# A frequency filter and gated FFN on one core: batch 0's D turned in SBUF, half of batch 1's A through DRAM, x chunks in the first x's buffers

## The chip, the cores and the metric

The kernel runs on one core of a Trainium2 chip. The metric is the device time of one execution in microseconds. All times within an execution are microseconds from the start of the profiled span. The engines are called PE (TensorE, matmul), DVE (VectorE), ACT (ScalarE), POOL (GpSimd) and SP (SyncE, which here only issues DMAs). [...]

## The reference

x has 8 batches of 3008 rows and 256 columns. Each batch is filtered in the frequency domain along its rows, and the 24064 filtered rows go through a gated feed-forward layer with 1536 hidden columns:

```python
X = np.fft.rfft(x, axis=1)                    # x: (8, 3008, 256)
Y = X * (filt_r + 1j * filt_i)[None, :, :]
y = np.fft.irfft(Y, n=3008, axis=1)
t = y.reshape(24064, 256)
out = (np.maximum(t @ w_gate, 0.0) * (t @ w_val)) @ w_out
```

## The kernel before

**The filter as matmuls.** A row number is split, 3008 = N1 x N2 = 94 x 32. The transform of a batch has four stages. *A* is a transform over the 94 values for each of the 32 others; its result must then be turned, so that the 32 values lie along the partitions. The turned A is the tile `at`. `fwd(b, i)`, i from 0 to 5, takes `at` through the second transform (`F2`) into `psX`; `product` multiplies with the filter (`Ftr`, `Fti`) into `tt` and `uu`; `inv(b, i)` goes back through `I2t` and `I2u` into `psD`, and ACT copies that out as *D*. D must be turned as well, with the 94 frequencies' rows (96, `NROW`) on the partitions: the tiles `dC`. `item_c(k, h)` multiplies `dC` with `M1` (the way back over the 94) and gives `yT`, 512 columns of filtered x, transposed, for block k and half h of the 256 columns.

**How the two turns are done.** D goes to DRAM (`Dbuf`) as it stands and is read back in the other order: `inv` sends a DMA at the cuts 0, 2, 4, 6 (for batch 0 also 5), `load_d` reads it in four pieces z, two DMAs each. A of batches 2 to 7 is made by `tiled_a` from x chunks and goes through DRAM too (`Abuf`, `load_at_tiled`). A of batches 0 and 1 is made by `first_a` in 16 items (p, s, h), each one matmul in float32 (two instructions in the profile) and ACT's copy into `AS`, and turned by DVE with `turn_a`, in 32 x 32 blocks of 32-bit words (L301, STREAM_TRANSPOSE).

**The x chunks.** For a batch from 2 on, `load_chunk(b, j)` loads a quarter of x on POOL's queue into `XP[j]`, `fold_chunk` adds and subtracts its halves on POOL, `tiled_a(b, j)` transforms it. `XP` is four tiles of their own, cleared by POOL at step 2 (`clear_chunks`); `fold_chunk` keeps two of its four results in the tile `fold` (two buffers). The first x, of batches 0 and 1, is in `XF`, two tiles in the pool `pro`, which is closed ahead of the main loop.

**The FFN and the order.** 47 blocks of 512 rows, 12 steps each, 564 in all. A step is `gv`: two matmul pairs into `psV` and `psG`, ACT's copy `vsb`, DVE's `prod`; and a twelfth of the output stage `o_part` of the block before. The order on every engine is the order of the program. What belongs to the filter is put at the end of steps by `at_step`: `end` is the step five ahead of the `item_c` that first needs batch b (51 for batch 1, 123 for batch 2), and fwd, inv, `load_d`, `tiled_a` and the loads stand at fixed distances from it. `item_c` of the next block stands at the steps 8 and 10 of a block.

**The start.** x of batch 0 is loaded and transformed, the filters are loaded, `first_b` runs batch 0's six fwd, product and inv, with three items of batch 1's `first_a` between (`amid`). Then come 13 more items; on POOL, `hold_gpsimd` (a small copy that waits for what it reads) delays the first half of the gate and value weights (`load_vg`) until an item of batch 1 is copied, and the second half, the output weights (`load_o`) and two pieces of D until the first piece of `dC` has landed. `item_c(0, h)` and the main loop follow.

**PSUM** has eight banks, handed out in turn by `bank` and `done`.

Of the kernel before, what the change touches and what calls it, by code (L numbers as in the profile page):

```python
# [29 lines left out]
N1, N2 = 94, 32  # L30
# [11 lines left out]
def _tables():  # L42
    n1 = np.arange(N1)
    n2 = np.arange(N2)
    p = np.arange(16)
    wa = np.zeros((128, 128))
    part = 4 * (n1 % 32) + n1 // 32
    m1 = np.zeros((NROW, N1))
    f2 = np.zeros((128, NG, 64))
    lo = np.arange(64)  # L50
    lo = 32 * (lo // 32) + 4 * (lo % 8) + lo % 32 // 8
    own = np.zeros((128, 2, 2, 64))
    order = np.arange(64).reshape(2, 32).T.reshape(64)
    for hg in range(48):
        g, a = divmod(hg, 2)
        rows = slice(a * 64, a * 64 + 64)
        e, j = g % 2, 12 * a + g // 2
        rt, rm = 64 * e + j, 48 * e + j
        f = np.zeros((64, 64))
        t = np.zeros((64, 64))  # L60
        u = np.zeros((64, 64))
        k1 = 1 + g + 24 * a if hg != 47 else 0
        th = 2 * np.pi * (((n1 - 23) * k1) % N1) / N1
        wa[part, rt] = np.cos(th)
        if k1 not in (0, 47):
            wa[part, rt + 32] = -np.sin(th)
            m1[rm] = 2.0 * np.cos(th) / S
            m1[rm + 24] = -2.0 * np.sin(th) / S
            k = np.stack([k1 + N1 * p, S - (N1 * (p + 1) - k1)], 1).reshape(32)
            conj = np.tile([1.0, -1.0], 16)  # L70
            th = 2 * np.pi * (np.outer(n2, k) % S) / S
            c, s = np.cos(th), np.sin(th)
            f[:] = np.block([[c, -s], [s, c]])
            ct, st = c.T, s.T
            t[:] = np.block([[ct, st], [-st, ct]])
            u[:] = np.block([[-st, ct], [-ct, -st]]) * np.concatenate([conj, conj])[:, None]
        else:
            m1[rm] = np.cos(th) / S
            th = 2 * np.pi * (np.outer(n2, k1 + N1 * p) % S) / S
            c, s = np.cos(th), np.sin(th)  # L80
            f[0:32, 0:32:2] = c
            f[0:32, 32::2] = -s
            t[0:32:2, 0:32] = 2.0 * c.T
            t[32::2, 0:32] = -2.0 * s.T
            u[0:32:2, 0:32] = -2.0 * s.T
            u[32::2, 0:32] = -2.0 * c.T
            if k1 == 0:
                sign = np.where(n2 % 2 == 0, 1.0, -1.0)
                f[0:32, 32] = sign
                t[0, 0:32] = 1.0  # L90
                t[32, 0:32] = sign
                u[0] = 0.0
                u[32] = 0.0
        f2[lo + 64 * e, j] = f
        if g >= NG - 2:
            own[rows, 0, g - NG + 2], own[rows, 1, g - NG + 2] = t[:, order], u[:, order]

    r = np.arange(128)
    perm = np.zeros((128, 64))
    perm[r, 2 * (8 * (r % 4) + r // 4 % 8) + r // 32 % 2] = 1.0  # L100
    swap = np.zeros((128, 128))
    conj = np.where(r % 2 == 0, 1.0, -1.0)
    swap[r ^ 32, r] = conj * np.where(r & 32, -1.0, 1.0)
    m1 = np.concatenate([m1, np.zeros((128 - NROW, N1))])
    fold = np.zeros((128, 4, 32))
    i = np.arange(24)
    for odd in range(2):
        k1 = 2 - odd + 2 * (i % 12) + 24 * (i // 12)
        if not odd:
            k1[k1 == 48] = 0  # L110
        th = 2 * np.pi * (np.outer(i - 23, k1) % N1) / N1
        half = np.where(i == 23, 0.5, 1.0)[:, None]
        for q in range(4):
            fold[32 * q:32 * q + 24, 2 * odd, 0:24] = np.cos(th) * half
            fold[32 * q:32 * q + 24, 2 * odd + 1, 0:24] = np.where(k1 % 47 == 0, 0.0, -np.sin(th))
    tab = np.concatenate([perm, swap, own.reshape(128, -1), m1], 1)
    return wa.astype(np.float32), fold.reshape(128, 128).astype(np.float32), f2.astype(NBF16), tab.astype(NBF16)
# [3 lines left out]
def kernel(  # L121
# [44 lines left out]
    Abuf = [dram.tile([NROW * N2, D], BF16, name=f"Abuf{b}") if b > 1 else None for b in range(B)]  # L166
    Dbuf = [dram.tile([NROW * N2, D], BF16, name=f"Dbuf{b}") for b in range(B)]

    XF = [pro.tile([128, NX2 * D], FP32, name=f"XF{c}") for c in range(N2 // NX2)]
    WA = pro.tile([128, 128], FP32)  # L170
    AS = [[pro.tile([128, NC2, N2 // NC2, D // 2], BF16, name=f"AS{b}{h}")] for b, h in ((0, 0), (0, 1), (1, 0))]
    WF = consts.tile([128, 4, 32], FP32)
    M1 = consts.tile([NROW, N1], BF16)
# [46 lines left out]
    def place_own():  # L220

        for i, t in enumerate((I2t, I2u)):
            o = 192 + i * 128
            nc.vector.tensor_copy(t[64:, NG - 2:, :],
                                  tabs[64:, o:o + 128].rearrange("p (g n) -> p g n", g=2))
        nc.vector.tensor_copy(M1, tabs[:NROW, 448:])

# [49 lines left out]
    def first_a(b, p, s, h):  # L277
# [6 lines left out]
        if len(AS) == 3 and (b, h) == (1, 1):  # L284
# [7 lines left out]
    def turn_a(b, h, i=0, d0=0, d1=None):  # L292

        if (h, i, d0) == (0, 0, 0):
            ats[b] = sb.tile([128, 32, D], BF16, tag="at", bufs=1, name="at")
# [5 lines left out]
        nc.vector.transpose(dst[:, o + d0:o + d1, :], src[:, d0:d1, :])  # L301

# [15 lines left out]
    def fold_chunk(b, j):  # L318

        xp = XP[j]  # L320
        t = fs.tile([128, 2, 512], FP32, tag="fold", bufs=2, name="fold")
        tt = nc.gpsimd.tensor_tensor
        tt(t, xp[:, 0:2], xp[:, 2:4], op=ALU.add)  # L323
        tt(xp[:, 2:4], xp[:, 0:2], xp[:, 2:4], op=ALU.subtract)  # L324
        tt(xp[:, 0], t[:, 0], t[:, 1], op=ALU.add)
        tt(t[:, 0], t[:, 0], t[:, 1], op=ALU.subtract)
        tt(t[:, 1], xp[:, 2], xp[:, 3], op=ALU.add)
        tt(xp[:, 2], xp[:, 2], xp[:, 3], op=ALU.subtract)
        fold[b, j] = (xp[:, 0], t[:, 0], t[:, 1], xp[:, 2])
# [66 lines left out]
    def inv(b, i, cuts=CUTS):  # L396

        if i in cuts:
            if (b, i) == (0, 5):
                dsb = AS[0][0].rearrange("p (a o) c d -> p a (o c d)", a=2)  # L400
                dsb = dsb.rearrange("p a (o d) -> p a o d", d=D)
            else:
                dsb = sb.tile([128, 2, 4, D], BF16, tag="dsb", bufs=3, name="dsb")
            dsbs[b] = i, dsb
        i0, dsb = dsbs[b]
# [10 lines left out]
        o = 2 * (i - i0)  # L416
        for a in range(2):
            copy = nc.vector.tensor_copy if (b, i, a) == (0, 5, 0) else nc.scalar.copy
            copy(dsb[:, a, o:o + 2, :], psD[a])  # L419
            done(psD[a])  # L420
        if i + 1 in cuts:
            nc.sync.dma_start(_ap(Dbuf[b], 2 * i0 * D, [[NG * D, 128], [NG // 2 * D, 2], [1, (o + 2) * D]]),
                              dsb[:, :, :o + 2, :])

    def first_b(amid):

        cuts = (0, 2, 4, 5, 6)
        for i in range(6):
# [6 lines left out]
            if i > 1:  # L435
                inv(0, i - 2, cuts=cuts)
            amid(i)
        inv(0, 4, cuts=cuts)
        amid(6)
        inv(0, 5, cuts=cuts)  # L440

    dCs = {}

    def load_d(b, z0=0, z1=NZ, engs=(nc.sync, nc.sync)):
        for z in range(z0, z1):
            dC = sb.tile([NROW, 8, D], BF16, tag="dC", bufs=6)
            for e in range(2):
                engs[e].dma_start(dC[48 * e:48 * e + 48],
                                  _ap(Dbuf[b], (64 * e + 16 * z) * NG * D,
                                      [[D, 48], [48 * D, 8], [1, D]]))  # L450
            dCs[b, z] = dC
# [13 lines left out]
    def item_c(k, h):  # L465
# [4 lines left out]
        for (o, b, n2, n1, w) in runs(k * W, W):  # L470
            nc.tensor.matmul(psY[:, o:o + w],  # L471
                             dCs[b, n2 // 8][:, n2 % 8, h * 128:(h + 1) * 128], M1[:, n1:n1 + w],
# [103 lines left out]
    for i in range(3):  # L576
        make_back_u(i)
    for h in range(2):
# [4 lines left out]
    place_filter(1, 0, 0, nc.gpsimd.tensor_copy)  # L583
    for fi, a, half in ((0, 0, 0), (0, 1, 0), (1, 1, 0), (0, 0, 1), (0, 1, 1), (1, 0, 1), (1, 1, 1)):
        place_filter(fi, a, half, nc.sync.dma_start)
    load_x(1, sp, ((0, 0, 2 * q), (0, 2 * q, 4 * q), (1, 0, 2 * q), (1, 2 * q, 4 * q)))
    early = iter([(0, s, h) for h in range(2) for s in range(2)] +
                 [(p, s, h) for h in range(2) for p in range(1, 4) for s in range(2)])

    def amid(i):  # L590
# [4 lines left out]
        for _ in range((0, 0, 0, 0, 1, 1, 1)[i]):  # L595
            first_a(1, *next(early))

    first_b(amid)
    for _ in range(3):
        p, s, h = next(early)  # L600
        first_a(1, p, s, h)
    hold_gpsimd(AS[2][0][:, 4 * s, p, 0:8])
    load_vg(0, DFF // 2)
    load_d(0, 0, 2)
    hold_gpsimd(dCs[0, 0][:, 7, D - 8:])
    load_vg(DFF // 2, DFF)
    load_o()
    load_d(0, 2, 4, (nc.gpsimd, nc.gpsimd))
    for p, s, h in early:
        first_a(1, p, s, h)  # L610
        if (p, s, h) == (3, 1, 0):
            turn_a(1, 0)
    for h in range(2):
        item_c(0, h)
# [3 lines left out]
    XP = []  # L618

    def clear_chunks():  # L620
        for i in range(4):
            XP.append(fs.tile([128, 4, 512], FP32, tag=f"XP{i}", bufs=1, name=f"XP{i}"))
            nc.gpsimd.memset(XP[i], 0.0)

# [6 lines left out]
    for k in range(4):  # L631
        at_step((5, 11, 14, 16)[k], lambda k=k: turn_a(1, 1, k // 2, k % 2 * 16, k % 2 * 16 + 16))
    at_step(2, clear_chunks)
    for b in range(1, B):
        end = (b * S // W - 1) * NFT + C_AT[0] - 5
        if b > 1:
            for j, e in enumerate((-74, -69, -62, -55) if b == 2 else (-74, -69, -64, -57)):
                l = (22, 29, 34, 43)[j] if b == 2 else end - 115 + NFT * j
# [11 lines left out]
        for i in range(7):  # L650
            l = -33 + 5 * i if b == 1 else -40 + 6 * i
# [6 lines left out]
        at_step(end - (1 if b == 1 else 2), lambda b=b: load_d(b))  # L658
# [42 lines left out]
```

## Time and profile before

| | us |
|---|---|
| median of 3 runs (lowest, highest) | 889.12 (887.46, 891.44) |
| the profiled execution | 888.4 |
| its span | 886.3 |
| PE busy, in the span | 863.7 |
| DVE, ACT, POOL busy | 573.8, 500.7, 373.5 |
| the first fwd of batch 0 (psX) | 27.0 |
| the last inv of batch 0 (psD) | 39.0 |
| the first matmul of the FFN (psV) | 53.8 |
| the first fwd of batch 1, step 18 (psX) | 75.2 |
| the last inv of batch 1, step 48 (psD) | 121.3 |

The table of windows gives for a stretch its length, then the busy time of PE, weight load, DVE, ACT and POOL, the granted clock of PE, the DMA share (busy share of the 16 DMA engines; above 1 where several transfers overlap on them) and GB/s. The granted clock was 1.00 in every stretch looked at. In the timeline a line is: start, duration, engine, line, operation, written tile, read tiles, shape, count, and in brackets the engine's idle time before it with what ended it. "SPq" and "POOLq" are the engines' queues of DMA issues: the duration there is that of issuing.

### The profile page before, as it was taken

The page shows a single profiled execution, that of the slowest core. Times are in us where ns is not written, and L with a number is a line of the kernel's source. Part 1 is how long each engine was busy: PE and PEld are TensorE (multiplying, and loading weights), DVE is VectorE, ACT ScalarE, POOL GpSimd, SP SyncE. Part 2 cuts the span into 40 slices and gives each one's busy share as a digit, 9 for nine tenths or more (in the row PEclk, how much of TensorE's full clock was granted, in tenths as well). Part 3 has the DMA queues.
Part 4 walks back from the last instruction along what each step waited for, and adds up shares of the span by engine and source line. Part 5 has one row for each costly group of instructions (what it writes and reads, how often), then busy time and mean ns, then how long its engine had stood idle before and what let it go on. Part 6 is the DMA issues. An engine that isn't in the chain of part 4 may idle for free.

```text
span 886.3 us, 19058 instructions
## 1 busy us (share of the span) xinstructions
PE 863.7 (97%) x7071; PEld 508.0 (57%) x7193; DVE 573.8 (65%) x863; ACT 500.7 (56%) x905; POOL 373.5 (42%) x374
## 2 busy tenths in 40 slices
PE   8989999999999999999999999999999999999998
PEld 4336555566556665566655565556655556566665
DVE  3768765577666776667765676657776577655553
ACT  4765554555655565556565556555655555555553
POOL 6661795137641567316771167802867000000001
PEclk9999999999999999999999999999999999999999
DMA  9992466533466337543375234753446512321111
GB/s 238 282 177 49 137 155 139 133 101 113 116 155 137 102 102 165 130 112 101 105 190 131 81 100 129 182 118 84 118 133 150 123 31 81 91 65 36 38 31 54
DMA packets 105731, 104.41 MB, mean 118 GB/s; under 512 B 20215, under 2 KB 90391, under 8 KB 104966
## 3 DMA queue, kind: packets, MB, share of 16 engines
q1 hardware_dynamic: 82374, 75.21, 33.3%
q0 software_dynamic: 22864, 27.19, 13.1%
q8 instruction: 57, 0.93, 0.5%
q10 hardware_dynamic: 400, 0.79, 0.3%
q14 instruction: 36, 0.29, 0.1%
HBM read 58.93 MB, written 46.66 MB: 119 GB/s over the span
## 4 chain that ended last, share of the span: by engine, by line
PE 85%; DMA 7%; DVE 2%; ACT 2%; issue 1%; POOL 1%; SPq 1%; POOLq 0%; DVEq 0%
PE psG L487 26%; PE psO L508 25%; PE psV L487 24%; PE psF L337 3%; PE psD L411 2%; PE psY L471 2%; DVE prod L492 2%; PE psX L374 2%; ACT vsb L490 2%; DMA dC<-Dbuf 2%; DMA at<-Abuf 1%; DMA XF<-in_x_dram 1%; DMA Fti<-in_filt_i_dram 1%; DMA Fti<-Fti 1%; DMA Dbuf<-dsb 1%
## 5 line engine op out<-in xcount | busy, mean ns | idle before, releaser
L492 DVE SCALAR_TENSOR_TENSOR prod<-psG,vsb 128x512 bf16<-128x512 f32 x564 | 388.7, 690 | 259.6 <-ACT vsb L490 253.2
L490 ACT CAST vsb<-psV 128x512 bf16<-128x512 f32 x564 | 331.9, 589 | 265.5 <-PE psV L487 137.4
L508 PE MATMUL psO<-WoT,prod 128*128 128x256 bf16 x2256 | 336.5, 273 | 1.1
L487 PE MATMUL psG<-yT,WgT 128*128 128x512 bf16 x1105 | 330.4, 379 | 5.8 <-DMA WgT<-in_moe_w_gate_dram 0.6
L487 PE MATMUL psV<-yT,WvT 128*128 128x512 bf16 x1031 | 315.9, 380 | 1.2 <-DVE yT L478 0.7
L508 PEld LDWEIGHTS <-prod 128*128 128x128 bf16 x2256 | 220.7, 98 | 143.3
L487 PEld LDWEIGHTS <-WgT 128*128 128x128 bf16 x1128 | 110.0, 98 | 135.6 <-issue 1.8
L487 PEld LDWEIGHTS <-WvT 128*128 128x128 bf16 x1128 | 98.3, 98 | 40.7 <-issue 29.5
L274 POOL CAST scr<-prod 128x8 f32<-128x8 bf16 x24 | 4.5, 190 | 254.7 <-DVE prod L492 254.7
L532 POOL DMA_DIRECT2D out_dram<-osb x5 | 2.6, 535 | 195.7 <-ACT osb L521 195.7
L521 ACT COPY osb<-psO 128x512 f32<-128x512 f32 x92 | 53.9, 586 | 25.8 <-PE psO L508 24.6
L390 DVE TENSOR_TENSOR tt<-psX,Ftr 128x512 bf16<-128x512 f32 x96 | 64.9, 681 | 1.6 <-PE psX L374 0.9
L323 POOL TENSOR_TENSOR fold<-XP 128x1024 f32<-128x1024 f32 x24 | 56.5, 2355 | 19.5 <-PE psF L337 19.3
L390 DVE TENSOR_TENSOR uu<-psX,Fti 128x512 bf16<-128x512 f32 x88 | 59.8, 680 | 0.0
L310 POOL DMA_DIRECT2D XP<-in_x_dram x96 | 56.6, 593 | 2.8 <-PE psY L471 1.4
L324 POOL TENSOR_TENSOR XP<-XP 128x1024 f32<-128x1024 f32 x24 | 56.4, 2349 | 1.9
L419 ACT CAST dsb<-psD 128x512 bf16<-128x512 f32 x94 | 50.6, 592 | 11.0 <-PE psD L411 11.0
L344 ACT CAST asb<-psF 128x512 bf16<-128x512 f32 x48 | 25.8, 589 | 30.1 <-PE psF L337 30.1
L344 DVE CAST asb<-psF 128x512 bf16<-128x512 f32 x48 | 30.9, 686 | 18.1 <-PE psF L337 17.3
L476 ACT CAST yT<-psY 128x512 bf16<-128x512 f32 x47 | 27.5, 586 | 26.1 <-PE psY L471 25.9
L471 PE MATMUL psY<-M,dC 96*128 96x94 bf16 (+18 forms) x604 | 37.7, 198 | 3.6 <-DMA dC<-Dbuf 3.6
L471 PEld LDWEIGHTS <-dC 96*128 96x128 bf16 x604 | 34.4, 97 | 7.9 <-issue 3.4
(73 smaller groups left out, 503.0 us busy)
## 6 DMA issues: line engine op xcount, KB each, us to landing
XP<-in_x_dram POOLq DMA_DIRECT2D x48, 256.0 KB, 6.0
Dbuf<-dsb SPq DMA_DIRECT2D x23, 512.0 KB
dC<-Dbuf SPq DMA_DIRECT2D x60, 192.0 KB
XP<-in_x_dram POOLq DMA_DIRECT2D x96, 96.0 KB, 2.7
Abuf<-asb SPq DMA_DIRECT2D x96, 96.0 KB
at<-Abuf SPq DMA_DIRECT2D x24, 384.0 KB
out_dram<-osb SPq DMA_DIRECT2D x69, 94.0 KB
XF<-in_x_dram SPq DMA_DIRECT2D x20, 256.0 KB
```

Source lines behind the costliest of these rows:

```text
L310: nc.gpsimd.dma_start(xp[r:r + 24, 0:4:2, :], _ap(x, (b * N1 * N2 + o) * D, [[N2 * D, 24], [47 * N2 * D, 2], [1, 512]]))
L323: tt(t, xp[:, 0:2], xp[:, 2:4], op=ALU.add)
L324: tt(xp[:, 2:4], xp[:, 0:2], xp[:, 2:4], op=ALU.subtract)
L344: copy(asf[:, :, q, :], banks[q])
L390: nc.vector.tensor_tensor(p, psX, filt, op=ALU.mult)
L419: copy(dsb[:, a, o:o + 2, :], psD[a])
L471: nc.tensor.matmul(psY[:, o:o + w], dCs[b, n2 // 8][:, n2 % 8, h * 128:(h + 1) * 128], M1[:, n1:n1 + w], start=True, stop=True)
L487: nc.tensor.matmul(pt[:, :W], w[:, h, ft * 128:(ft + 1) * 128], yt[:, h, :], start=(h == 0), stop=(h == 1))
L490: nc.scalar.copy(vsb, psV[:, :W])
L492: nc.vector.scalar_tensor_tensor(prod, in0=psG[:, :W], scalar=0.0, in1=vsb, op0=ALU.max, op1=ALU.mult)
L508: nc.tensor.matmul(psO[:, t % 2], prods[ft][:, t * 128:(t + 1) * 128], WoT[:, ft, :], start=(ft == 0), stop=(ft == NFT - 1))
L521: copy(osb[:, t0 % 2:t % 2 + 1], psO[:, t0 % 2:t % 2 + 1])
```

## The change

- **D of batch 0** isn't sent to DRAM. `inv` copies it into `AS0`, the tile that held batch 0's A (now one tile of 32 rows of D columns, of which 24 are used; POOL clears the other 8 after the turns of batch 0's A). `turn_d(h)` turns one half of its columns on DVE into `dCb`. The turn gives the rows of D in another order (32 to a block, 128 partitions), so `M1` has a second version for batch 0 and the tables of the way back (`perm`, `own`) no longer interleave the two halves of D's rows.
- **`dCb`**, one tile of 48 rows for D, takes the place of the six `dC` buffers; for batch 1's first half of A its last 16 rows serve as `AS`.
- Because the tables no longer interleave, **the store of D** of batches 1 to 7 puts its rows into place in DRAM by four DMAs, one for each 32 partitions, in place of one.
- **The weights** are loaded on POOL without the two holds, and no D on POOL's queue.
- **Half of batch 1's A** (h = 0) isn't turned by DVE: `store_half` and `load_half` take it through DRAM, four DMAs each on SP. The items of `first_a(1)` are all of h = 0 first, then h = 1; both `item_c(0, h)` stand ahead of the last item.
- **The other half's `turn_a`**: the first of four pieces ahead of the main loop, the rest at steps 4, 11 and 14 (before: 5, 11, 14, 16).
- **x chunks** in halves of the two `XF` tiles, which stay; nothing is cleared. `fold_chunk` leaves all four results in the chunk; `fold` has one buffer. Batch 2's chunks are loaded at steps 6, 14, 22, 30 (before: 22, 29, 34, 43), its last two `tiled_a` and its `load_at_tiled` stand two steps earlier.
- **Batch 1's fwd, product and inv** stand two steps earlier, its `load_d` one step.

```diff
-            m1[rm] = 2.0 * np.cos(th) / S
-            m1[rm + 24] = -2.0 * np.sin(th) / S
+            for l in range(2):
+                m1[rm[l], l] = 2.0 * np.cos(th) / S
+                m1[rm[l] + (24, 32)[l], l] = -2.0 * np.sin(th) / S
...
-    XF = [pro.tile([128, NX2 * D], FP32, name=f"XF{c}") for c in range(N2 // NX2)]
+    XF = [consts.tile([128, NX2 * D], FP32, name=f"XF{c}") for c in range(N2 // NX2)]
+    XP = [t[:, i * 2048:i * 2048 + 2048].rearrange("p (k d) -> p k d", d=512) for t in XF for i in range(2)]
     WA = pro.tile([128, 128], FP32)
-    AS = [[pro.tile([128, NC2, N2 // NC2, D // 2], BF16, name=f"AS{b}{h}")] for b, h in ((0, 0), (0, 1), (1, 0))]
+    AS0 = pro.tile([128, 32, D], BF16)
+    dCb = consts.tile([128, 48, D], BF16)
+    AS = [[t.rearrange("p n d -> p (n d)").rearrange("p (l c d) -> p l c d", l=NC2, d=D // 2)]
+          for t in (AS0[:, 0:16, :], AS0[:, 16:32, :], dCb[:, 32:48, :])]
...
+    def turn_d(h):
+
+        src = AS0.bitcast(FP32).rearrange("p k d -> p d k")
+        dst = dCb[:, 0:32, :].bitcast(FP32).rearrange("p n d -> p d n")
+        d = slice(h * D // 4, h * D // 4 + D // 4)
+        nc.vector.transpose(dst[:, d, :], src[:, d, :])
+
+    def store_half(b):
+        w = N2 * D // 2
+        for q in range(4):
+            nc.sync.dma_start(_ap(Abuf[b], q * NG * w, [[w, NG], [1, w]]),
+                              AS[2 * b][0][32 * q:32 * q + NG].rearrange("p l c d -> p (l c d)"))
+
+    def load_half(b):
+        w = N2 * D // 2
+        for q in range(4):
+            nc.sync.dma_start(ats[b][32 * q:32 * q + 32, 0:NG, 0:D // 2],
+                              _ap(Abuf[b], q * NG * w, [[D // 2, 32], [w, NG], [1, D // 2]]))
...
-        t = fs.tile([128, 2, 512], FP32, tag="fold", bufs=2, name="fold")
+        t = fs.tile([128, 2, 512], FP32, tag="fold", bufs=1, name="fold")
...
-            copy(dsb[:, a, o:o + 2, :], psD[a])
+            copy(dsb[:, a, o:o + 2, :] if b else AS0[:, 12 * a + 2 * i:12 * a + 2 * i + 2, :], psD[a])
             done(psD[a])
-        if i + 1 in cuts:
-            nc.sync.dma_start(_ap(Dbuf[b], 2 * i0 * D, [[NG * D, 128], [NG // 2 * D, 2], [1, (o + 2) * D]]),
-                              dsb[:, :, :o + 2, :])
+        if b and i + 1 in CUTS:
+            for q in range(4):
+                nc.sync.dma_start(_ap(Dbuf[b], (64 * (q // 2) + q % 2) * NG * D + 2 * i0 * D,
+                                      [[2 * NG * D, 32], [NG // 2 * D, 2], [1, (o + 2) * D]]),
+                                  dsb[32 * q:32 * q + 32, :, :o + 2, :])
...
     place_filter(1, 0, 0, nc.gpsimd.tensor_copy)
+    nc.gpsimd.memset(AS0[:, NG:, :], 0.0)
...
     first_b(amid)
-    for _ in range(3):
-        p, s, h = next(early)
-        first_a(1, p, s, h)
-    hold_gpsimd(AS[2][0][:, 4 * s, p, 0:8])
     load_vg(0, DFF // 2)
-    load_d(0, 0, 2)
-    hold_gpsimd(dCs[0, 0][:, 7, D - 8:])
     load_vg(DFF // 2, DFF)
     load_o()
-    load_d(0, 2, 4, (nc.gpsimd, nc.gpsimd))
-    for p, s, h in early:
+    for h in range(2):
+        turn_d(h)
+    new_at(1)
+    for p, s, h in items:
         first_a(1, p, s, h)
         if (p, s, h) == (3, 1, 0):
-            turn_a(1, 0)
-    for h in range(2):
-        item_c(0, h)
+            store_half(1)
+            load_half(1)
+        if (p, s, h) == (3, 0, 1):
+            for hh in range(2):
+                item_c(0, hh)
+    turn_a(1, 1, 0, 0, 16)
...
-    for k in range(4):
-        at_step((5, 11, 14, 16)[k], lambda k=k: turn_a(1, 1, k // 2, k % 2 * 16, k % 2 * 16 + 16))
-    at_step(2, clear_chunks)
+    for k in range(1, 4):
+        at_step((4, 11, 14)[k - 1], lambda k=k: turn_a(1, 1, k // 2, k % 2 * 16, k % 2 * 16 + 16))
...
-            for j, e in enumerate((-74, -69, -62, -55) if b == 2 else (-74, -69, -64, -57)):
-                l = (22, 29, 34, 43)[j] if b == 2 else end - 115 + NFT * j
+            for j, e in enumerate((-74, -69, -64, -57)):
+                l = (6, 14, 22, 30)[j] if b == 2 else end - 115 + NFT * j
...
-            l = -33 + 5 * i if b == 1 else -40 + 6 * i
+            l = -35 + 5 * i if b == 1 else -40 + 6 * i
...
-        at_step(end - (1 if b == 1 else 2), lambda b=b: load_d(b))
+        at_step(end - 2, lambda b=b: load_d(b))
```

## The prediction

> **What bounds the kernel now.** First the page's sums, then the table of windows, to see where TensorE is not fed.
>
> ```profile
> span 886.3 us, 19058 instructions
> PE 863.7 (97%) x7071; PEld 508.0 (57%) x7193; DVE 573.8 (65%) x863; ACT 500.7 (56%) x905; POOL 373.5 (42%) x374
> 40.00:60.00 20.00, 17.46 (x63) 7.57 (x62) 9.15 (x9) 12.67 (x29) 8.66 (x13) 1.00 1.01 203
> 120.00:140.00 20.00, 17.96 (x179) 9.73 (x181) 10.66 (x17) 10.89 (x20) 19.43 (x17) 1.00 0.90 193
> 160.00:180.00 20.00, 19.09 (x130) 11.52 (x132) 11.35 (x18) 9.96 (x18) 3.88 (x7) 1.00 0.66 151
> 287.00:394.00 107.00, 106.15 (x910) 62.80 (x926) 71.97 (x112) 61.54 (x111) 54.73 (x52) 1.00 0.50 125
> ```
>
> PE (TensorE) idles 22.6 of 886.3 us. From 287 to 394 it idles 0.85 us in 107, so a change can gain only where PE waits: 2.54 us in 40 to 60, 2.04 in 120 to 140, 0.91 in 160 to 180. The timeline (start, duration, what; in brackets the idle time before and its releaser) and the chain of waits (start, length, what) say for what, in the first of them:
>
> ```profile
> 39.57 11.43 PE L282 MATMUL psA<-XF,WA 128*128 128x512 f32 x26
> 46.50 4.28 DVE L301 STREAM_TRANSPOSE at<-AS 128x2048 f32<-128x2048 f32 x1 [6.13 <-ACT AS L289]
> 52.76 0.62 PE L471 MATMUL psY<-M,dC 96*128 96x94 bf16 x12 [1.77 <-DMA dC<-Dbuf]
> 53.83 0.72 PE L487 MATMUL psV<-yT,WvT 128*128 128x512 bf16 x2 [0.44 <-ACT yT L476]
> 60.37 0.61 PE L487 MATMUL psG<-yT,WgT 128*128 128x512 bf16 x2 [0.64 <-DMA WgT<-in_moe_w_gate_dram]
> 75.20 0.41 PE L374 MATMUL psX<-at,F 64*64 64x256 bf16 x8
> ```
>
> ```profile
> 40.43 4.99 DMA Dbuf<-AS
> 45.86 6.76 DMA dC<-Dbuf
> 53.90 6.42 DMA WgT<-in_moe_w_gate_dram
> ```
>
> D of batch 0 goes out for 4.99 us and comes back for 6.76; behind it, held on POOL by the copy that reads dC, the second half of the gate weights is 6.42 us on its way. PE covers the round trip with 13 first_a items (26 matmuls in 11.43 us, 0.86 an item), then waits 1.77, 0.44 and 0.64 us. PE's waits from 60 to 180 us give the other two stalls:
>
> ```profile
> PE psY L471 <- DMA dC<-Dbuf: 1.9, 1, 1.9
> PE psX L374 <- DMA at<-Abuf: 0.8, 1, 0.8
> ```
>
> The first is batch 1's D (at 135 to 137), the second batch 2's A (at 176).
>
> **The change, part by part.**
>
> *D of batch 0 in SBUF.* Four Dbuf stores and eight dC loads vanish; instead DVE turns AS0 in two pieces. Price: the two L301 transposes of this size at 18.70 took 8.23 us together, one took 4.28. They can start when inv(0, 5) has been copied (40.4), so the halves are ready at 44.6 and 48.7. DVE did nothing there but one turn_a (46.50), which is removed. PE reaches item_c(0, 0) after 12 of the 13 items: 39.57 + 12 x 0.863 = 49.9, so the turns are hidden with 1.2 us to spare; were that gone, item_c(0, 1) waits one for one. Two item_c take 0.62, to 50.55; the 13th item runs 0.86 to 51.4 and covers the copies of yT (0.58 and 0.69). The FFN loop starts at 51.45 and not 53.83: **-2.4**.
>
> *Weights.* With both holds gone POOL issues all six loads when its products end (38.3), 0.7 to 0.8 us each, done at 43. From 54.0 to 67.5 the same kind of traffic moved 2.37 MB in 13.4 us, so they land by about 53; the second gate half is needed at step 6 (51.45 + 6 x 0.86 = 56.6), WoT at 62.3. PE's idle time in 59 to 61 goes: 0.28 + 0.37 = **-0.65**. They share the DMA engines with x of batch 1, which items now need 1.7 us earlier (its last quarter at 42.2). 28.5 to 36.5 us moved 2.1 MB; the 1.2 MB left take 3.2 us at the 380 GB/s of 38 to 41, to 39.7, because the Dbuf traffic is away. Bounds 0 and 0.6 (the rest at half that rate, 42.8); I take 0, since POOL's first load is only issued at 38.3.
>
> *The memset of AS0's rows 24 to 31 on POOL.* It stands ahead of POOL's products, back to back from 28.20 for 6.92 us and on the chain, and must wait for the second turn (26.93). The row at L553 gives 1.81 us for 2048 elements of 32 bits; this one has 2048 of 16. Bounds: 0 (half, done at 27.9) and 0.65 (as L553). I take 0: the zero memsets of bf16 at L561 ran as 32-bit words, half as many.
>
> *Batch 1's first half through DRAM.* It saves DVE 4.28 us that nobody waited for, and puts eight DMAs on SP, idle then: four stores after item 8 (43.9, copied by 44.6), 0.52 each, landing within 5 us (the 4.99 above), so 49.6 to 51.6; then four loads, 3072 runs of 256 B. Queued behind is WF alone, wanted at 123. The nearest rows are batch 3's load of as many runs of 512 B, issued at 264.96, with DMA busy until 274, so 9.2 us, and batch 2's 9.11. That lands at 59 to 61, with the weights' tail and the first x chunk (from 57) beside it up to 64. Step 18's psX stood at 75.20; step 16 lies 2 x 1.30 earlier and moves with the 2.8 gained until then (2.4 + 0.65 - 0.25, below), so PE wants the half at 69.8. Bounds: 0 (5 us to spare) and +3 (twice the time, 67 to 73). I take 0, by the row.
>
> [...]
>
> *turn_a of the other half.* One piece (1.21 us) stands ahead of the first prod, the next at step 4. In steps 0 to 11 DVE needs 0.69 of each 0.86 us, and PE may lead by about 1.6 us before it lacks banks (eight, two a step). Bounds 0 and 0.7; I take **+0.25**, the size of PE's wait for DVE at 66.2.
>
> *Batch 1 two steps earlier.* fwd at 16 to 41, load_d at 49 ahead of the Abuf stores. The last inv stands two steps (psD 121.3 to 118.1) earlier; the wait at 136.9 was 1.87: **-1.9**. *Batch 2's chunks at 6 to 30*, the last two tiled_a and load_at two steps (2.6 us) earlier: the wait of 0.81 goes, **-0.8**. POOL's four memsets (7.1 us) and its waits for a second fold buffer go too, worth nothing: POOL is not on the chain.
>
> *Four stores instead of one per cut of D.* SP issues nine more DMAs per batch, 0.52 each.
>
> ```profile
> 232.50 0.52 SPq L422 DMA_DIRECT2D Dbuf<-dsb  x1
> 239.46 5.45 SPq L448 DMA_DIRECT2D dC<-Dbuf  x8
> 244.54 0.41 PE L471 MATMUL psY<-M,dC 96*128 96x8 bf16 x7
> ```
>
> The whole store lands after 6.9 us here (3.9 in batch 7), and load_d waits for that on SP. The last quarter goes out 1.56 later; a 96 KB chunk lands in 2.7, so 4.3 in all. Bounds -2 and +1.6 on the landing. PE used batch 2's D 5.1 us after the load without a wait, batches 3 to 7 after 5.8 to 7.8: at worst 1.6 is felt in batch 2 and 0.9 in batch 7. I take 0.
>
> **Sum:** -2.4 - 0.65 - 1.9 - 0.8 + 0.25 = -5.5. The profiled execution took 888.4 (span 886.3 and 2.1 around it), which gives 882.9. The median, 889.12, lies 0.7 higher: **883.6**.
>
> **Rivals.**
> 1. *The half is somewhat late.* Runs of 256 B take about twice those of 512 B, and PE waits at step 16 for up to 5 us. For: DMA share is about 1 for most of 46 to 67 before, and the chunk comes into it. Against: the 5 us to spare. 885 to 888.5.
> 2. *Other side: the half is very late.* Same place; each us past 69.8 costs one. It decides from 75 on, where it eats all 5.5: the loads would need 25 us from their first issue, over 2.5 times batch 3's, if the weights' and the chunk's traffic went ahead of them throughout. Landing at 80.5 to 82.5 makes 894 to 896. Against: the weights alone should be through by 53.
> 3. *The loop doesn't start earlier.* x and the weights hold each other up, or the memset costs its 0.65 and DVE's second turn ends late: 1.5 to 2 of the 2.4 stay. For: 1.2 us of cover is little. 885.5.
> 4. *The split stores land later.* Batch 1's stall stays in part (1) and batches 2 and 7 pay 2.5 in all. For: batch 2's slack isn't seen, only that it is not negative. 886 to 887.
>
> **Chances.** Forecast 0.58, rivals 0.12, 0.09, 0.11, 0.10. A measurement here tells about 0.5% from no change, 4.4 us: faster means below 884.7, slower above 893.6. Of the forecast 0.53 lies below 884.7, of rivals 3 and 4 0.02: faster 0.55. Of rival 2, 0.07 lies above 893.6; the rest, 0.38, is between. The forecast's own range is 882 to 885 (the spread of the runs below it, 1.4 of the unknown costs above). The range of 8 in 10 reaches to rivals 1, 3 and 4: 881 to 889, a us below for the spread of the runs before (887.46 to 891.44); it leaves out rival 2 and little else.
>
> **What would show it.** Right: no Dbuf or dC transfer before 100 us; two transposes between 40.4 and 49; the first psV near 51.4; no PE wait for WgT, none at the psY near 130 nor at the psX near 170; PE idle in 40 to 60 below 0.5. Wrong: a PE wait for at or Abuf near 69 (rivals 1, 2); psA waiting for XF or psY for DVE around 42 to 50 (3); psY waiting for dC at batches 1, 2 or 7 (4). The forecast falls if PE's idle time in the first 180 us doesn't shrink by about 5 us.

## The result and the profile after

| | before | after |
|---|---|---|
| median, us (lowest, highest) | 889.36 (886.71, 891.71) | 894.41 (892.38, 895.45) |
| ratio, 95% interval | | 1.0058 [1.0040, 1.0077] |
| span of the profiled execution | 886.3 | 892.1 |
| its first psX (first fwd of batch 0) | 26.98 | 26.02 |
| its first psV (the FFN loop starts) | 53.83 | 53.07 |
| its first psO (output stage, step 12) | 66.87 | 75.53 |

The changed kernel is slower by 0.6%; 883.6 was forecast, and 894.41 lies above the range too. What stands ahead of the first psX differs from run to run without regard to the kernel (25.8 to 27.0 over all traces of this study), so stretches are counted from there. From the first psX to the first psO the kernel before took 39.89 us, the changed one 49.51: **9.6 us lost**. From the first psO to the end it took 819.4 before and 816.6 after: **2.9 us gained**, close to the 2.7 that the prediction had for that part. The head is 1.0 shorter, and the three add up to the 5.8 between the spans.

First the sums of the changed kernel's profile, then the two largest waits of PE and the one of DVE that is new.

```profile
span 892.1 us, 19099 instructions
PE 866.5 (97%) x7072; PEld 509.0 (57%) x7193; DVE 579.6 (65%) x864; ACT 501.3 (56%) x905; POOL 365.3 (41%) x365
PE psG L509 <- DVE prod L514: 7.4, 1, 7.4
PE psD L428 <- DVE uu L413: 1.8, 1, 1.8
```

```profile
DVE at L302 <- DMA at<-Abuf: 9.7, 1, 9.7
```

PE's three waits that the change was to take away (dC at 136.9, `at` at 176, WgT at 60.4) are gone. In their place PE waits once for 7.4 us, and not for a DMA but for DVE's `prod`; DVE in turn stood for 9.7 us until a DMA into `at` had landed. The chain of waits (start, length, what) names that DMA:

```profile
47.25 6.43 DMA Abuf<-dCb
...
53.70 1.02 SPq L323
...
54.81 7.80 DMA at<-Abuf
...
62.73 0.06 DVE at L302
...
63.83 0.66 DVE prod L514
...
64.53 1.01 PE psG L509 x2
```

The path goes through `store_half` and `load_half`: half of batch 1's A on its way through DRAM. It landed at 62.6, near the 59 to 61 of the prediction and 7 us ahead of the 69.8 at which the prediction had step 16 read it (in this run step 16 came at 81.3). What waits for it is DVE's instruction on L302, the first piece of `turn_a(1, 1)`, which stands ahead of the main loop. It reads batch 1's other half of A (`asb`) and writes the other 128 columns of the same tile `at`, so no datum is exchanged between the two; but the program makes the second writer of the tile wait for the first (the 9.7 us above; in e3 below, with two tiles, there is no such wait). All `prod` of the FFN stand behind that piece on DVE. PE goes on for four and a half steps, until the next `psG` needs a bank that a `prod` must free, and stops at 57.1.

The table of windows shows what that stop does to TensorE itself (length; busy time of PE, weight load, DVE, ACT, POOL; granted clock; DMA share; GB/s):

```profile
57.00:58.00 1.00, 0.12 (x1) 0.00 (x0) 0.00 (x0) 0.00 (x0) 0.00 (x0) 1.00 1.24 193
59.00:60.00 1.00, 0.00 (x0) 0.00 (x0) 0.00 (x0) 0.00 (x0) 0.00 (x0) 0.99 1.24 176
60.00:61.00 1.00, 0.00 (x0) 0.00 (x0) 0.00 (x0) 0.00 (x0) 0.00 (x0) 0.50 1.12 133
64.00:65.00 1.00, 0.47 (x2) 0.20 (x2) 1.00 (x3) 0.44 (x1) 0.00 (x0) 0.50 0.03 8
69.00:70.00 1.00, 1.00 (x3) 0.29 (x2) 0.69 (x1) 0.16 (x1) 0.12 (x1) 0.50 0.00 0
70.00:71.00 1.00, 1.00 (x6) 0.45 (x5) 0.39 (x1) 0.46 (x2) 0.49 (x2) 0.89 0.00 0
```

From 60, 2.9 us after PE stopped, the granted clock is 0.50, and it stays there until 70.2, 5.7 us after PE has work again: busy, but at half speed: a pair of `psV` matmuls (L509), 0.59 us at 56.5, takes 1.06 at 67.0. The busy share alone would miss this.

The 1.8 us that psD waits for DVE's `uu` is a second loss, at 26 to 30, in the timeline:

```profile
26.00 0.19 DVE L227 COPY I2t<-tabs 64x128 bf16<-64x128 bf16 x1
26.09 1.85 POOL L607 MEMSET AS<- 128x2048 bf16 x1 [1.43 <-DVE at L302]
26.11 1.87 DVE L227 COPY I2u<-tabs 64x128 bf16<-64x128 bf16 x1
27.99 2.26 POOL L411 TENSOR_TENSOR uu<-xs,Fti 128x512 bf16<-128x512 f32 x2
28.00 1.21 DVE L229 COPY M<-tabs 128x188 bf16<-128x188 bf16 x1
29.12 0.68 DVE L413 TENSOR_TENSOR tt<-psX,Ftr 128x512 bf16<-128x512 f32 x1
```

and in the kernel before:

```profile
27.07 0.19 DVE L224 COPY I2u<-tabs 64x128 bf16<-64x128 bf16 x1
27.43 0.69 DVE L390 TENSOR_TENSOR tt<-psX,Ftr 128x512 bf16<-128x512 f32 x1
```

In the changed kernel two copies have one form and size: the first, just ahead of POOL's memset, takes 0.19 us, the second, beside it, 1.87, and ends with it (27.98 and 27.94). The next copy takes 1.21 and ends where the first of POOL's two products, 1.13 each, does; before the change the three took 0.19 each. DVE's first `tt` starts 3.10 after the first psX, before 0.45. The `tt` themselves keep their length: 0.68 in the changed kernel, beside POOL's product, and 0.69 before.

### The profile page after: what moved, and what is told of

It is laid out like the page before. It is cut to its first block, busy times and chain, and to the rows that moved or that the text cites. A ratio compares the mean times of both kernels' runs of the same rounds, so it can differ in the third digit from the quotient of the medians.

```text
span 892.1 us, 19099 instructions
## 1 busy us (share of the span) xinstructions
PE 866.5 (97%) x7072; PEld 509.0 (57%) x7193; DVE 579.6 (65%) x864; ACT 501.3 (56%) x905; POOL 365.3 (41%) x365
## 4 chain that ended last, share of the span: by engine, by line
PE 89%; DMA 4%; DVE 2%; ACT 1%; issue 1%; POOL 1%; SPq 0%; DVEq 0%; POOLq 0%
PE psG L509 28%; PE psO L530 26%; PE psV L509 25%; PE psF L360 3%; PE psD L428 2%; PE psY L492 2%; PE psX L397 2%; DVE prod L514 2%; ACT vsb L512 1%; DMA at<-Abuf 1%; PE psA L285 1%; DMA Fti<-in_filt_i_dram 1%; DMA XF<-in_x_dram 1%; DMA Abuf<-dCb 1%; DMA Fti<-Fti 1%
## 5 line engine op out<-in xcount | busy, mean ns | idle before, releaser
L509 PE MATMUL psG<-yT,WgT 128*128 128x512 bf16 x1107 | 332.5, 380 | 12.6 <-DVE prod L514 7.4
L509 PE MATMUL psV<-yT,WvT 128*128 128x512 bf16 x1030 | 316.9, 381 | 0.9 <-DVE yT L500 0.6
L509 PEld LDWEIGHTS <-WgT 128*128 128x128 bf16 x1128 | 110.4, 98 | 143.0 <-issue 10.8
L509 PEld LDWEIGHTS <-WvT 128*128 128x128 bf16 x1128 | 98.7, 98 | 42.5 <-issue 32.3
L543 ACT COPY osb<-psO 128x512 f32<-128x512 f32 x92 | 54.0, 586 | 25.8 <-PE psO L530 24.0
L333 POOL DMA_DIRECT2D XF<-in_x_dram x96 | 56.9, 597 | 3.3 <-PE psY L492 1.5
L346 POOL TENSOR_TENSOR fold<-XF 128x1024 f32<-128x1024 f32 x24 | 57.2, 2384 | 0.7
L347 POOL TENSOR_TENSOR XF<-XF 128x1024 f32<-128x1024 f32 x24 | 56.5, 2352 | 1.9
L438 ACT CAST dsb<-psD 128x512 bf16<-128x512 f32 x84 | 45.1, 589 | 10.9 <-PE psD L428 10.9
L367 ACT CAST asb<-psF 128x512 bf16<-128x512 f32 x48 | 25.8, 589 | 29.0 <-PE psF L360 29.0
L492 PE MATMUL psY<-M,dCb 96*128 96x94 bf16 (+19 forms) x604 | 37.5, 198 | 0.0
L492 PEld LDWEIGHTS <-dCb 96*128 96x128 bf16 (+1 forms) x604 | 34.5, 97 | 3.3 <-issue 0.8
```

The lines of the kernel that those rows point to most:

```text
L333: nc.gpsimd.dma_start(xp[r:r + 24, 0:4:2, :], _ap(x, (b * N1 * N2 + o) * D, [[N2 * D, 24], [47 * N2 * D, 2], [1, 512]]))
L367: copy(asf[:, :, q, :], banks[q])
L438: copy(dsb[:, a, o:o + 2, :] if b else AS0[:, 12 * a + 2 * i:12 * a + 2 * i + 2, :], psD[a])
L492: nc.tensor.matmul(psY[:, o:o + w], dCs[b, n2 // 8][:, n2 % 8, h * 128:(h + 1) * 128], M1[:, 1, n1:n1 + w] if b == 0 else M1[:NROW, 0, n1: ...
L509: nc.tensor.matmul(pt[:, :W], w[:, h, ft * 128:(ft + 1) * 128], yt[:, h, :], start=(h == 0), stop=(h == 1))
L543: copy(osb[:, t0 % 2:t % 2 + 1], psO[:, t0 % 2:t % 2 + 1])
```

## The experiments

Every kernel below is the changed one with the edit shown; the times of kernels listed under one heading come from one chip, and each ratio is to runs of the kernel before on that chip. The stretch from the first psX to the first psO ("the stretch" from here on: 39.89 before, 49.51 after) is read from the profile of each.

**e1 to e4**, on one chip. Theory: DVE's wait for the load into `at` is the main loss, with the clock as its consequence; the memset is the second. Rival: the memset, or DMA traffic, is the main one.

e1 leaves out the clearing of AS0's rows 24 to 31, so these hold batch 0's A where the changed kernel has zeros; rows of zeros in `M1` multiply them.

```diff
-    nc.gpsimd.memset(AS0[:, NG:, :], 0.0)
```

> The changed kernel without POOL's clearing of AS0's rows 24 to 31; they keep batch 0's A, and meet only zero rows of M1. Theory (the clearing holds DVE): in the changed kernel DVE's copy into I2u takes 1.87 us from 26.11, ending with POOL's 1.85 us clearing, and the copy into M1 takes 1.21 us, ending with POOL's first product; before, they took 0.19 each. Without the clearing both are back at 0.2 to 0.3, the first tt comes 0.5 us after the first psX and not 3.1, and all after it 2.6 us earlier: 891 to 892.5 against the 894.4 of the changed kernel. Rival (the larger M1, 188 columns for 94, is what costs): I2u's copy may shorten, M1's stays at 1.2, under 1.5 us gained. Rival (nothing is gained, since the FFN waits for the half of A that comes from DRAM, and that is bound by DMA): the head is earlier, the landing of the half is not, and the time stays at 894.

Measured: 890.90 us, ratio 1.0034 [1.0017, 1.0051]; the stretch 46.80, 2.7 below the changed kernel. The psD wait for DVE is gone and the copy into the larger M1 takes 0.21 us without the memset (read in e6's trace), so its size is not what costs; DVE's wait for `at` (10.1) and PE's for `prod` (7.8) remain. So the memset is a cost, and the smaller one.

e2 keeps the order of the four pieces of `turn_a(1, 1)`, but puts them at steps 12 to 15.

```diff
-    turn_a(1, 1, 0, 0, 16)
...
-    for k in range(1, 4):
-        at_step((4, 11, 14)[k - 1], lambda k=k: turn_a(1, 1, k // 2, k % 2 * 16, k % 2 * 16 + 16))
+    for k in range(4):
+        at_step((12, 13, 14, 15)[k], lambda k=k: turn_a(1, 1, k // 2, k % 2 * 16, k % 2 * 16 + 16))
```

> The changed kernel with the four pieces of turn_a(1, 1) at steps 12, 13, 14 and 15, none ahead of the loop. Theory (DVE stands in its first piece until load_half has landed, at 62.6 in the changed kernel, with all prods behind it): no DVE wait for at over 1 us, PE's 7.4 us wait for prod and the half clock behind it (60 to 70) are gone, 9 to 10 us less: 884 to 886, with up to 1 us given back where four pieces in four steps make DVE late. Rival (the load from DRAM is itself too late, runs of 256 bytes): PE or DVE waits for at at step 12 to 16 for 3 us or more and the time is 887 to 891. Rival (the PE idle time is not DVE's doing but the banks'): no gain, 894.

Measured: 886.24 us, 0.9976 [0.9961, 0.9990]; the stretch 39.15. With the memset still there, moving the pieces behind the landing takes 10.4 us out of the stretch, as much as e3 below, which leaves them where they are; it gives 1.7 back at step 16, where psX waits for DVE: the four pieces, 1.17 to 1.20 us each, and a `prod` of 0.64 after each fill DVE from 66.5 to 73.1, while PE starts a step every 1.30.

e3 takes the reason for the wait away: the half is loaded into a tile of its own, and batch 1's `fwd` reads its columns in two matmuls of 128 and not one of 256.

```diff
+    at1 = consts.tile([128, NG, D // 2], BF16)
...
-            nc.sync.dma_start(ats[b][32 * q:32 * q + 32, 0:NG, 0:D // 2],
+            nc.sync.dma_start(at1[32 * q:32 * q + 32],
...
-                    nc.tensor.matmul(psXs[b, i, e][64 * a:64 * a + 64, m],
-                                     F2[64 * e:64 * e + 64, j, :],
-                                     ats[b][64 * e:64 * e + 64, j, :], start=True, stop=True,
-                                     tile_position=(64 * e, 64 * a))
+                    for t, c0, c1 in [(ats[b], 0, D)] if b != 1 else [(at1, 0, D // 2), (ats[b], D // 2, D)]:
+                        nc.tensor.matmul(psXs[b, i, e][64 * a:64 * a + 64, m, c0:c1],
+                                         F2[64 * e:64 * e + 64, j, :],
+                                         t[64 * e:64 * e + 64, j, c0:c1], start=True, stop=True,
+                                         tile_position=(64 * e, 64 * a))
```

> The changed kernel with load_half into a tile of its own, 24 rows of 128 columns; fwd of batch 1 takes its two halves in two matmuls of 128 columns each. The pieces of turn_a stay where they are. Theory (the piece waits only because it writes the same tile as the load, into other columns): the first piece runs at 53 to 55 without a wait for DMA, PE's 7.4 us wait is gone and the clock stays at 1.0; the doubled matmuls of six fwd cost under 1 us; 884.5 to 887. Rival (DVE can't write beside such a DMA, or the piece needs the loaded data): the wait of 9.7 us stays and so does the time, 894 to 895.

Measured: 883.99 us, 0.9953 [0.9939, 0.9968]; the stretch 39.16. The order of the program, the pieces and the transfers' source are those of the changed kernel; the tile is another, and with it the split of batch 1's matmuls, which come after the stretch. DVE's wait and PE's are both gone, and of PE's waits the largest left is the memset's:

```profile
PE psD L431 <- DVE uu L416: 1.8, 1, 1.8
```

So the 10.35 us between 49.51 and 39.16 come from two writers of one tile, and nothing waited for the half itself.

e4 asks what part of these is the clock. It keeps the wait and gives PE 34 matmuls whose result nobody uses, at step 2, to bridge the idle time.

```diff
             gv(k, ft, prods)
+            if (k, ft) == (0, 2):
+                psJ = bank("psJ", 512)
+                for _ in range(34):
+                    nc.tensor.matmul(psJ, WgT[:, 0, 0:128], WgT[:, 0, 0:512], start=True, stop=True)
+                done(psJ)
```

> The changed kernel with 34 matmuls of 512 columns, whose result nobody reads, on PE between steps 2 and 3: 7.3 us of work in place of 7.4 us of idling. DVE's wait stays. Theory (the idle time costs twice, the second time by a granted clock of 0.50 until 70): the clock stays at 1.0 and about 3 us are saved, 891 to 892. Rival (the half clock is hidden behind DVE's backlog of prods): the clock stays at 1.0 and the time at 894; if the filler ends late, up to 1 us more.

Measured: 892.09 us, 1.0055 [1.0038, 1.0073]; the stretch 47.19. In the table of windows of e4:

```profile
60.00:64.00 4.00, 4.00 (x21) 1.77 (x19) 0.93 (x1) 0.00 (x0) 0.00 (x0) 1.00 0.61 73
64.00:68.00 4.00, 3.42 (x16) 1.53 (x16) 4.00 (x7) 2.34 (x4) 0.00 (x0) 1.00 0.01 2
```

The clock stays at 1.00 through the wait, and the stretch is 2.3 us shorter than after's: by these two traces that is the price of the clock, and the wait itself costs the other 8 (47.19 against 39.16 in e3). The price isn't fixed: against c_after below, the changed kernel once more, the stretch of e4 is only 1.0 shorter. The ratio does not tell e4 from the changed kernel (1.0055 against 1.0058), so the price of the clock rests on single profiles. e4's own has a lower clock early (0.87 from 27 to 40) that cost nothing that shows: psX to psV is 27.06, in after 27.05.

**c_after, c_before, e5, e6**, on another chip. c_after and c_before are the two kernels once more.

> The changed kernel itself, unchanged, timed beside the next ones. Its ratio to the kernel before was 1.0058 (1.0040 to 1.0077); 1.004 to 1.008 again. From the first psX of batch 0 to the first psO its trace took 49.5 us (75.53 - 26.02), the kernel before 39.9; 49.5 within 0.3 again, if that distance is a property of the program.

> The kernel before itself, for a second trace: its first psX stood at 26.98, those of five traces of the changed kernel and its variants at 26.02 to 26.36. Theory (the loads of x at the start vary from run to run): anywhere from 26.0 to 27.0, and first psX to first psO 39.9 within 0.3. Rival (the change makes the head 0.7 us shorter): 26.9 to 27.1.

Measured: c_after 894.16 us, 1.0067 [1.0043, 1.0091], with DVE's wait for `at` 9.9 and PE's for `prod` 7.6 again. The stretch is 48.23, and not the 49.5 within 0.3 that was expected: the waits are the same, but the granted clock stands at 0.50 for about 6.8 us (its mean from 60 to 80 is 0.83, and it is back near 68.5, from where a pair on L509 takes 0.59 us again) and not for 10.2 (60.0 to 70.2). c_before, one execution: 888.09 us, the first psX at 25.82 (26.0 to 27.0 was expected), the stretch 39.62. The earlier psX of the changed kernel is thus no gain of it.

e5 joins e1 and e2, e6 joins e1 and e3.

> The changed kernel without the clearing of AS0 and with the four pieces of turn_a(1, 1) at steps 12 to 15. Theory (two separate losses, 2.7 us by DVE's held copies and 10 by the piece that waits for the load): 2.1 to 2.7 less than with the late pieces alone, so first psX to first psO 36.5 us, and the ratio 0.9945 to 0.997. Rival (the landing of the half, not DVE, then sets the pace): the pieces at step 12 wait for at by over 1 us, and the ratio is 0.997 to 0.999.

> The changed kernel without the clearing and with load_half into a tile of its own, the pieces of turn_a where the change has them. Theory (with both losses gone the terms of the prediction stand: 2.4 + 0.65 ahead of step 12, 1.9 and 0.8 later): first psX to first psO 36.5 us, 3.4 below the kernel before; no wait for Abuf or Dbuf at batches 1 and 2; 6 us under the kernel before, ratio 0.992 to 0.994. Rival (the early start of the FFN is given back where batch 1's half lands, or at the split stores): the same 36.5, but a PE wait at step 16 or at a psY, and 0.994 to 0.997.

Measured: e5 883.25 us, 0.9942 [0.9921, 0.9962], the stretch 36.50, with 1.8 us of psX waiting for DVE. e6 **881.55 us, 0.9923 [0.9901, 0.9944]**, the stretch 36.51, no wait for DVE's pieces. Without its two losses the change does about what was forecast of it: −5.5 us was forecast, here the time goes from 888.61 to 881.55, and in the next group from 887.26 to 881.32. e6 is faster than the kernel before and the changed one.

**e7, e8, e9 and e6 again**, on one chip. e7 is e3 (memset kept, own tile) with the copies of L227 and L229 on ACT:

```diff
-            nc.vector.tensor_copy(t[64:, NG - 2:, :],
+            nc.scalar.copy(t[64:, NG - 2:, :],
...
-        nc.vector.tensor_copy(M1, tabs[:, 448:].rearrange("p (l n) -> p l n", l=2))
+        nc.scalar.copy(M1, tabs[:, 448:].rearrange("p (l n) -> p l n", l=2))
```

> The half of batch 1's A in a tile of its own, as in e6, and POOL clears AS0's rows again, but the two copies of the tables in bf16 (I2u and M1) are made by ACT and not by DVE. Theory (POOL's clearing costs time only because it holds DVE's bf16 copies, and not as work on POOL): from the first psX to the first psO 36.5 us, as in e6, and a ratio to before of 0.992 (about 881.5 us); DVE's first tt within 0.6 us of ... its psX; ACT's copies 0.3 to 0.7 us each, not 1.2 to 1.9. Rival (the clearing holds DVE's products too, or delays POOL's products by 0.9 to 1.8): 37.4 to 39.2 us and 0.993 to 0.995 (882.5 to 884.3 us), as in e3 (39.2 us, 0.9953).

Measured: 881.69 us, 0.9941 [0.9924, 0.9957]; the stretch 37.02, against 36.76 of e6 on this chip and 36.51 before. The timeline of e7:

```profile
26.17 0.41 PE L400 MATMUL psX<-at,F 64*64 64x256 bf16 x8 [0.34 <-DVE at L302]
26.24 1.80 POOL L610 MEMSET AS<- 128x2048 bf16 x1 [2.56 <-DVE at L302]
26.62 0.69 DVE L416 TENSOR_TENSOR tt<-psX,Ftr 128x512 bf16<-128x512 f32 x1 [0.50 <-PE psX L400]
28.09 2.27 POOL L414 TENSOR_TENSOR uu<-xs,Fti 128x512 bf16<-128x512 f32 x2
```

The memset is as long as before (1.80 us, in after 1.85), and DVE's first `tt` starts 0.45 after psX and takes 0.69 in the middle of it: the memset holds DVE's bf16 copies (I2u's took 1.87 beside it in after) and not its `tt`. That POOL's product starts 1.92 after psX and not 1.22 (before) is what is left of the cost here, 0.3 to 0.5 (PE's waits for POOL's `uu` are 1.0 in all, in e6 0.4). On ACT the copies ran at 24.3 to 25.2, ahead of the memset, so whether ACT's copies would be held beside it was not seen.

e8 and e9 undo one move each in e6.

```diff
-            for j, e in enumerate((-74, -69, -64, -57)):
-                l = (6, 14, 22, 30)[j] if b == 2 else end - 115 + NFT * j
+            for j, e in enumerate((-74, -69, -62, -55) if b == 2 else (-74, -69, -64, -57)):
+                l = (22, 29, 34, 43)[j] if b == 2 else end - 115 + NFT * j
```

> e6 with batch 2's chunks loaded at the steps 22, 29, 34 and 43 and its last two tiled_a and load_at two steps later, as before the change. If the prediction's term of 0.8 for this move is right, PE waits for at of batch 2 at its first psX for about 0.8 us again, and the time is 0.8 above e6 (882.4 us, ratio 0.9932). Rival (the wait had gone for another reason, the loads being earlier for the freed queues): no such wait, time as e6 (0.9923).

```diff
-            l = -35 + 5 * i if b == 1 else -40 + 6 * i
+            l = -33 + 5 * i if b == 1 else -40 + 6 * i
...
-        at_step(end - 2, lambda b=b: load_d(b))
+        at_step(end - (1 if b == 1 else 2), lambda b=b: load_d(b))
```

> e6 with batch 1's fwd, product and inv two steps later and its load_d one step later, as before the change. If the prediction's term of 1.9 is right, PE waits for dCb of batch 1 at the first psY after 120 us for 1.9 to 2.5 us again, and the time is about 1.9 above e6 (883.5 us, ratio 0.9945). Rival (the loop's earlier start or the four stores had taken the wait away): a wait below 0.5 us and the time of e6 (0.9923).

> e6 once more, on the same chip as e7, e8 and e9. Every theory: a ratio to before of 0.990 to 0.994 (about 881.5 us), 36.5 us from the first psX to the first psO.

Measured: e6 again 881.32 us, 0.9938 [0.9922, 0.9955]. e8 883.84 us, 0.9959 [0.9941, 0.9978], 2.5 above e6 and not 0.8. e9 881.84 us, 0.9940 [0.9924, 0.9957], 0.5 above and not 1.9, less than the intervals can tell. The waits of PE in e8:

```profile
PE psX L400 <- DMA at<-Abuf: 1.9, 1, 1.9
PE psY L495 <- DMA dCb<-Dbuf: 1.0, 1, 1.0
```

Late chunks bring **both** waits back, also the one for batch 1's D; e9 has neither. (This profile is of an execution of 886.09 us, 2.3 above e8's median, so these waits and what follows them add up to more than the median's 2.5.) Below are the eight issues of batch 1's `load_d` on SP (start, length): in the kernel before, in e8, in e6's second run and in e9.

```profile
129.64 6.46 SPq L448 DMA_DIRECT2D dC<-Dbuf  x8
120.15 11.35 SPq L473 DMA_DIRECT2D dCb<-Dbuf  x8
120.37 6.85 SPq L473 DMA_DIRECT2D dCb<-Dbuf  x8
123.60 4.68 SPq L473 DMA_DIRECT2D dCb<-Dbuf  x8
```

POOL issues batch 2's last chunk from 121.9 on in the kernel before, from 118.0 in e8, from 95.2 in e6 and from 94.7 in e9. e8 and e6 start the D load at the same point; with the late chunk its issues end at 131.5, with the early one at 127.2. e9 starts them 3 us later than e6 and ends at 128.3, still without a wait. So the chunks' early place is enough to free batch 1's D (e9), and the earlier start of the D load alone is not: it leaves 1.0 us (e8) of the 1.9 before (2.5 in c_before's trace). That the chunk's loads hold up the issues is read from these traces and not shown by itself: e8 also moves two `tiled_a` and a `load_at_tiled`, and e6 and e9 differ by 2.2 us with the chunk equally far ahead.

## Why the prediction was wrong

**The step that failed: "*turn_a of the other half.*"** It put one piece ahead of the first prod and priced it at +0.25 us, by DVE's load. The part on batch 1's half asked what is queued behind the four loads on SP ("WF alone") and when PE wants the half, but not who else touches the tile that they write. The piece does, and with it every `prod`. Measured (after against e3): 10.35 us in the place of 0.25, of which 8.0 are the wait, 7.4 of them PE's idle time, and, by e4's profile, 2.3 the clock. With the profile of c_after it is 9.1; the ratios of the times (1.0058 and 1.0067 against 0.9953) make it 9.3 to 10.1. That PE may lead by about 1.6 us was in the prediction; a wait of 9.7 on DVE against it was not.

The clock's part, as measured: in the trace of after it is 0.50 from 2.9 us after PE's stop until 5.7 us after PE has work again, in c_after until 2.8 us after. In e8 the clock fell for a stop of only 1.9 us (last section).

**The second: "*The memset of AS0's rows 24 to 31 on POOL.*"** It was priced at 0, at most 0.65, as a delay of POOL's products, on half the time of a 32-bit clear. The row that it took for the half, L561, is of memsets on DVE, which show there as 32-bit words (64x256 uint32); on POOL the clear ran as 2048 bf16 elements. It took 1.85 us, as long as the 32-bit row on POOL (1.81, L553), and cost 2.7 (e1 against after; e6 against e3 the same 2.65). Only 0.3 to 0.5 of that came over POOL's products (e7 against e6); the rest came over DVE's bf16 copies, which the prediction did not look at, though they stood in the timeline at the same microseconds. In after the copy into I2u took 1.87 us beside the memset's 1.85 and ended 0.04 after it; in e7 a `tt` beside the memset took 0.69, as without it. Why the copy is held and the `tt` is not, no run shows.

**What held.** *D of batch 0 in SBUF*, −2.4: psX to psV 26.85 before, 24.40 in e6, −2.45 (24.66 in its second run, −2.2), with both turns of DVE in 40.4 to 47.7 (44.6 and 48.7 were forecast as their ends). *Weights* and the first steps, −0.65 + 0.25 = −0.40: psV to psO 13.04 before, 12.10 in e6, −0.94, more than forecast; the wait for WgT is gone, and the pieces, once free, cost nothing that shows. *The half through DRAM* at 0: it landed at 62.6 against 59 to 61, 10.4 us after its first issue, where the row of as many 512-byte runs had 9.2. So a run of 256 B took about as long as one of 512, and a byte about twice as long, with the weights loading beside it; PE never waited for it. That the half's runs would take twice the time, the bound of +3 and the condition of rival 1, was the author's estimate and is not what was measured. *Four stores per cut* at 0: no wait of psY for dCb from batch 2 on, in after or e6.

**Right in sum by luck, wrong in parts:** *batch 1 two steps earlier*, −1.9, and *batch 2's chunks*, −0.8. Undone in e6, the first costs 0.5, which the intervals don't tell from nothing (e9), the second 2.5 (e8), near the 2.7 of both. The prediction read the wait for batch 1's D as a matter of when its load starts; with the chunks early a later start brought no wait, and with the chunks late the earlier start did not remove it.

**The rivals.** Rivals 1 and 2 had the half late at PE's step 16; it was on time, and hurt through DVE at step 0. Rival 2's time, 894 to 896, was met by another mechanism, so by chance. Rival 3 had the memset, but through DVE's second turn. Rival 4 did not come. None of the four had a wait of DVE for a transfer in it, though DVE's order ahead of the loop was what the change edits.

The windows of e6 (in its second run) show what the prediction had in mind; against the kernel before, PE's busy time rises from 17.46 to 19.95, 17.96 to 19.84 and 19.09 to 19.84:

```profile
40.00:60.00 20.00, 19.95 (x83) 9.10 (x83) 16.04 (x15) 14.49 (x34) 2.81 (x5) 1.00 1.09 202
120.00:140.00 20.00, 19.84 (x205) 10.57 (x177) 12.99 (x20) 11.70 (x22) 0.00 (x0) 1.00 0.72 163
160.00:180.00 20.00, 19.84 (x155) 11.96 (x157) 13.26 (x20) 10.89 (x20) 3.94 (x7) 1.00 0.35 94
```

## What to carry to other kernels

When a transfer is given a new target, list every instruction that writes or reads that tile, other columns too, and find the first of them in each engine's order; the load here was early enough for its reader and held another writer for 9.7 us, and a tile of its own was the cure (e3). Price what a new POOL instruction holds on DVE, not only on POOL: here a small bf16 copy beside it took 1.87 us for 0.19. And before crediting a vanished DMA wait to an earlier start, look at what other queues issue beside it: undoing each move alone (e8, e9) put 2.5 us on the move that was credited with 0.8.

## What the runs showed of the hardware

The clock also fell for a stop much shorter than after's. In e8 PE waited 1.91 us, from 171.2 to 173.1, and then:

```profile
172.00:173.00 1.00, 0.00 (x0) 0.00 (x0) 0.00 (x0) 0.00 (x0) 0.00 (x0) 1.00 0.59 89
173.00:174.00 1.00, 0.88 (x8) 0.44 (x9) 0.53 (x1) 0.00 (x0) 0.00 (x0) 0.72 0.45 154
175.00:176.00 1.00, 1.00 (x6) 0.62 (x5) 0.55 (x1) 0.11 (x1) 0.00 (x0) 0.50 0.60 172
177.00:178.00 1.00, 1.00 (x8) 0.65 (x7) 0.33 (x1) 0.59 (x1) 0.00 (x0) 1.00 0.14 46
```

By these windows (and 0.57 from 176 to 177) the clock is at half for 3.4 us, from about 173.4, which takes an estimated 1.7 us of work, for a wait of 1.9. The wait of 1.87 for dC in the kernel before, and the 1.0 at 131 in e8, left the clock at 1.00. But in c_before, the second trace of the kernel before, the same wait is 2.5 us long, and the mean clock is 0.93 from 120 to 140 and 0.99 from 140 to 160, an estimated 3.2 us at half. So of these waits of 1.9 to 2.5 us one cost nothing more and the one in e8, by the estimate, nearly double, and two executions of one kernel differed in it.

The times at half clock: 10.2 us in after (60.0 to 70.2) and 3.4 in e8, from windows of 1 us; and, estimated from the mean clock of longer windows as if it were either 1.00 or 0.50, 10.4 in e1 (0.92 from 40 to 60, 0.82 from 60 to 80), 6.8 in c_after (0.83 from 60 to 80), 3.2 in c_before and, ahead of the loop, 3.4 in e4 (0.87 from 27 to 40). What sets these lengths no run shows.

A bf16 memset of 2048 elements a partition took POOL 1.85 us (after, L607), as long as the 1.81 of one with 32-bit elements (before, L553).
